# Combinations of w_in and low halves of x on GpSimd, with a new order of work, in an attention and MoE kernel on one core

## The chip, the core and the metric

The kernel runs on one core of a Trainium2 chip. A core has five engines that matter here, each with its own queue of instructions that it executes strictly in order: TensorE (PE in the profile, with its weight loads as PEld), VectorE (DVE), ScalarE (ACT), GpSimd (POOL) and SyncE (SP), from which nearly all DMA transfers are issued. Engines wait for one another by semaphores. The metric is the device time of one execution in microseconds (us), from the first to the last instruction and what lies around them; lower is better.

## The reference

Attention with positive random features over 8 batches, 8 heads, 576 tokens and 64 channels, followed by a feed-forward layer with an unusual gate:

```python
def phi(x):
    proj = np.einsum('bhsd,df->bhsf', x, w_phi)
    proj = proj - np.max(np.abs(proj), axis=-1, keepdims=True)
    return np.concatenate([np.exp(proj), np.exp(-proj)], axis=-1)
q_p, k_p = (phi(q), phi(k))
kv = np.einsum('bhsf,bhsd->bhfd', k_p, v)
num = np.einsum('bhsf,bhfd->bhsd', q_p, kv)
den = np.einsum('bhsf,bhf->bhs', q_p, np.sum(k_p, axis=2))[..., None] + 1e-06
x = num / den            # to (4608 tokens, 512)
h = x @ w_in             # w_in 512 x 2048
sp = np.maximum(h, 0.0) + np.log1p(np.exp(-np.abs(h)))
g = h * erf(sp)
out = g @ w_out          # w_out 2048 x 512
```

## The kernel before

**Precision.** The large products run on TensorE in float16. Each float32 operand is split in two float16 parts, a high half (the rounded value, made by ScalarE or by a cast on VectorE) and a low half (value minus high half, one subtraction), and a product takes three matmuls: high by high, high by low, low by high.

**The first product** x @ w_in is done with seven products of blocks in place of eight (a scheme of Strassen's kind). It needs combinations of blocks of w_in and of blocks of x. The combinations of w_in are made once: the columns are handled in four units u = 0 to 3, each in two row blocks j = 0, 1. `split_weights(u, j)` (line 503) loads two tiles with `single` (line 474, which assembles float32 words from loaded 64-bit ones with three operations on lines 478, 480 and 482), makes four differences of 128x256 elements with the helper `tt` (line 520, called four times, so 32 in all), and then turns seven forms into high halves (an ACT operation recorded on line 442) and low halves (lines 530 and 531). The forms of unit 0 stay in SBUF (tile `wi`); those of units 1 to 3 are written to DRAM and fetched again for every stage.

**The stages.** x comes in nine stages s = 0 to 8 (eight batches of 512 tokens, and one stage of the 64 left-over tokens of each batch). For each stage, `split(s, f, ...)` (line 778) is called for seven forms f: the high half is cast on line 783 (ACT, stages 0 and 1) or 785 (DVE), the low half is subtracted on line 788 (128x512 elements), and SyncE issues a transposing DMA (line 789) that lays the result into an `x` tile. Some combinations of x are made by `combine` (line 812). A kind `x` of tiles may hold at most XS slots at once. The attention of pairs of heads p runs beside the products of earlier stages; from pair 12 on, q and k are split too, by `halve(p, i)` (line 598; low half on line 606, two per pair).

**Who does what.** Constants at the top choose the engine. `X_POOL = 0, 3` puts the low halves of x of stages 0 to 2 on GpSimd and the others on VectorE. `HL_POOL = 8, 16` puts the low halves of q and k of pairs 12 to 15 (the split starts at 12) on GpSimd. `T_POOL = 4` tells that the differences of w_in of all four units count as GpSimd's. But the helper `tt` refers to the variable `eng` of `split_weights`, and the loop below it assigns that variable anew, before any instruction is issued:

```python
pool = u < T_POOL
eng = nc.gpsimd if pool else nc.vector
tt = lambda ...: op(POOL if pool else DVE, 750 if pool else 330, lambda: eng.tensor_tensor(...), ...)
...
for f, x, c, key in (...):
    ...
    pool = u in LI_POOL and f in LF_POOL      # LI_POOL is empty
    eng = nc.gpsimd if pool else nc.vector
```

So the order of work is laid out as if GpSimd made the 32 differences in 750 ns each, and the instructions are issued on VectorE at those places in its queue.

**The order of work.** Every operation is first entered in a plan (`Plan.op`, line 149) with an engine, a counted length in ns, its reads and writes, and a priority (a position along TensorE's work, moved by offsets). `Plan.run` (line 199) then simulates the engines with these lengths, picks the next operation by time and priority, gives out tile slots, and issues all instructions in the order of planned start. An operation marked `port=True` may not start in the plan while one on the other of VectorE and GpSimd that is so marked is running. Where the plan expects a hole of more than 600 ns on TensorE, it fills it with pairs of matmuls on constant data (`warm`, line 1178), which compute nothing that is used. TensorE's work has three modes of how the array is used, and the plan adds 92 ns at a change and a penalty to the priority of an operation that would change it: STAY (1500) in the first steps, STAY2 (9000) in steps after N1. The weights are loaded one item at a time by `load_weight` (line 485), up to W_EARLY of them during the attention of the first batch, with a position moved by W_OFF; one of the steps of the product then follows another (`moe_step`, line 1088).

Of the kernel before, what the change touches and what calls it, by code (L numbers as in the profile page):

```python
# [13 lines left out]
ALU = mybir.AluOpType  # L14
# [25 lines left out]
PE_TURNED = 10  # L40
SPEED = {}
STAY2 = 9000.0
N1 = 9
TWO = 36
ATTN = 5
QK_POOL = 0, 0
W_POOL = 0, 0
GATE_AT = 0.0, 0.0, 0.0
X_POOL = 0, 3
T_POOL = 4  # L50
LO_POOL = ()
LI_POOL = ()
LF_POOL = 0, 1, 2, 3, 4, 5, 6
XC_POOL = 0, 0
HL_POOL = 8, 16
LATE = 1500.0
FIRST = 2
XS = 12
XT = 3
RES = 1  # L60
WS = 8
# [2 lines left out]
BIG = 20  # L64
HALF = 22
N0 = 6
W_EARLY = 4
W_NS = 1600.0
W_NS2 = 9000.0
ACC_AHEAD = 5000.0  # L70
# [6 lines left out]
W_FROM = 14  # L77
W_EACH = 7
W_MM = 14
W_OFF = 5000.0  # L80
W_AHEAD = 12000.0
X_AHEAD = 4000.0
SEVEN = 7
# [39 lines left out]
class Plan:  # L123
# [22 lines left out]
    def buf(self, kind):  # L146
        return Buf(self, kind)

    def op(self, eng, cost, fn, r=(), w=(), done=None, off=0.0, mode=COLS, land=0.0, port=False, need=None, give=None):
        o = Op()  # L150
        o.eng, o.cost, o.fn, o.mode, o.land, o.port = eng, cost, fn, mode, land, port
        o.slack = self.slack
        o.need, o.give = need, give
        o.stay = self.stay
        o.done = cost + 120.0 if done is None else done
        o.prio = self.pos + off
        o.seq = len(self.ops)
        o.succ, o.unmet, o.ready, o.start = [], 0, 0.0, None
        o.bufs = []
        deps = {}  # L160

        def touch(item, write):
            b, key = item if isinstance(item, tuple) else (item, None)
            if b not in o.bufs:
                o.bufs.append(b)
                b.left += 1
            known = write
            for k, (ws, rs) in b.state.items():
                if k is None or key is None or k == key:
                    known = True  # L170
                    for d in ws:
                        deps[d] = True
                    if write:
                        for d in rs:
                            deps[d] = True
            assert known, "read before it is written"
            if write:
                if key is None:
                    b.state.clear()
                b.state[key] = ([o], [])  # L180
            else:
                b.state.setdefault(key, ([], []))[1].append(o)

        for item in r:
            touch(item, False)
        for item in w:
            touch(item, True)
        deps.pop(o, None)
        for d in deps:
            d.succ.append(o)  # L190
        o.unmet = len(deps)
        self.ops.append(o)
        return o
# [125 lines left out]
def favor_attention_moe(ctx: ExitStack, tc: tile.TileContext, qk, vp, wphi, w_in, w_out, out):  # L319
# [6 lines left out]
    def slots(group, n, shape, dt):  # L326
        for i in range(n):
            plan.slot(group, f"{group}{i}", sb.tile(shape, dt, tag=f"{group}{i}", name=f"{group}{i}"))
# [48 lines left out]
    slots("half", HALF, [P, 512], F32)  # L377
    plan.kind("x", "half", (("x",), XS))
    plan.kind("xt", "half", (("xt",), XT))
# [24 lines left out]
    op, buf = plan.op, plan.buf  # L404
    PE, DVE, ACT, POOL, SP = "PE", "DVE", "ACT", "POOL", "SP"
# [52 lines left out]
    def wform(u, f):  # L458
        if u < RES:
            b = const[f"wi{u}"]  # L460
            return b, f, lambda hl, j: b.t[:, f, hl, j, :]
        b = wforms[u][f // 2]
        return b, f, lambda hl, j: b.t.bitcast(F16).rearrange("p (f h j n) -> p f h j n", f=2, h=2, j=2)[:, f % 2, hl, j, :]
# [21 lines left out]
    def load_weight():  # L485
        item = wq.pop(0)
        loaded.add(item)
        at_pos = plan.pos
        plan.pos += W_OFF
        if item[0] == "o":  # L490
# [12 lines left out]
    def split_weights(u, j):  # L503
        if u >= RES and j == 0:
            wforms[u] = [buf("ws") for _ in range(4)]
        rows = []
        for c in (j, 2 + j):
            st, f = buf("wr"), buf("wf")
            src = []
            for i in range(2):  # L510
                cols = slice(2 * (i * 8 + 2 * u) * P, 2 * (i * 8 + 2 * u + 2) * P)
                src.append((lambda st, i=i: st.t.bitcast(I32)[:, i * 512 : i * 512 + 512], w_in[c * P : (c + 1) * P, cols]))
            single(src, SP, st, f)
            rows.append(f)
        a, b = rows
        s, t = buf("wf"), buf("wf")
        lo, hi = slice(0, Q), slice(Q, 2 * Q)
        pool = u < T_POOL
        eng = nc.gpsimd if pool else nc.vector
        tt = lambda o, oc, x, xc, y, yc, r: op(POOL if pool else DVE, 750 if pool else 330, lambda: eng.tensor_tensor(o.t[:, oc], x.t[:, xc], y.t[:, yc], op=ALU.subtract), r=r, w=[(o, oc.start)], port=True)  # L520
        tt(s, lo, a, hi, a, lo, [a])
        tt(s, hi, b, hi, a, hi, [a, b])
        tt(t, lo, b, hi, s, lo, [b, (s, 0)])
        tt(t, hi, b, lo, t, lo, [b, (t, 0)])
        for f, x, c, key in ((B11, a, lo, a), (T3, s, hi, (s, Q)), (B21, b, lo, b), (T2, t, lo, (t, 0)), (T1, s, lo, (s, 0)), (B22, b, hi, b), (T4, t, hi, (t, Q))):
            w, k, view = wform(u, f)
            act(340, lambda view=view: view(0, j), lambda x=x, c=c: x.t[:, c], AF.Copy, [key], [(w, (k, j, 0)) if u < RES else (w, (f, j))], scale=SWI)
            pool = u in LI_POOL and f in LF_POOL
            eng = nc.gpsimd if pool else nc.vector
            op(POOL if pool else DVE, 800 if pool else 330, lambda eng=eng, view=view, x=x, c=c: eng.scalar_tensor_tensor(  # L530
                view(1, j), x.t[:, c], SWI, view(0, j), op0=ALU.mult, op1=ALU.subtract), r=[key, (w, (k, j, 0)) if u < RES else (w, (f, j))], w=[(w, (k, j, 1)) if u < RES else (w, (f, j))], port=True)
        if u >= RES and j == 1:
            wstored[u] = []
            for i in range(4):
                d = buf("wd")
                d.left += 1
                w = wforms[u][i]
                n = 512 * min(2, FORMS - 2 * i)
                op(SP, 430, lambda d=d, w=w, n=n: nc.sync.dma_start(d.t[:, :n], w.t[:, :n]), r=[w], w=[d], done=4000, land=1300 * LAND * n / 512)
                wstored[u].append(d)  # L540
# [57 lines left out]
    def halve(p, i):  # L598
# [4 lines left out]
        op(ACT, 100 + 0.85 * n, lambda: nc.scalar.copy(hv()[:, 0, cols], src.t[:, cols]), r=[src], w=[(hl, (i, 0))], off=-AHEAD)  # L603
        pool = HL_POOL[0] <= p < HL_POOL[1]
        eng = nc.gpsimd if pool else nc.vector
# [172 lines left out]
    def split(s, f, view, reads):  # L778
        t, x = buf("xt"), buf("x")
        xs[s, f] = x  # L780
        tv = lambda i: t.t.bitcast(F16).rearrange("p (t i d) -> p t i d", t=2, i=2)[:, :, i, :]
        if XT_ACT[0] <= s < XT_ACT[1]:
            op(ACT, 540, lambda: nc.scalar.copy(tv(0), view()), r=reads, w=[(t, 0)])
        else:
            op(DVE, 350, lambda: nc.vector.tensor_copy(tv(0), view()), r=reads, w=[(t, 0)], port=True)
        pool = X_POOL[0] <= s < X_POOL[1]
        eng = nc.gpsimd if pool else nc.vector
        op(POOL if pool else DVE, 1400 if pool else 600, lambda: eng.tensor_tensor(tv(1), view(), tv(0), op=ALU.subtract), r=[*reads, (t, 0)], w=[(t, 1)], port=True)
        op(SP, 1280, lambda: nc.sync.dma_start_transpose(
            x.t.bitcast(F16).rearrange("p (n t) -> p n t", t=P), t.t.bitcast(F16)), r=[t], w=[x], done=3100, land=600)  # L790
        if 1 < FIRST and s < FIRST:
            d = xds[s, f] = buf("xd")
            op(SP, 430, lambda: nc.sync.dma_start(d.t, x.t), r=[x], w=[d], done=4000, land=1300 * LAND, off=3000.0)
# [18 lines left out]
    def combine(s, out, x, y, sub, r, w):  # L812
        pool = XC_POOL[0] <= s < XC_POOL[1]
        eng = nc.gpsimd if pool else nc.vector
        op(POOL if pool else DVE, 1400 if pool else 600, lambda: eng.tensor_tensor(out(), x(), y(), op=ALU.subtract if sub else ALU.add), r=r, w=w, port=True)

    def first_half(s, a, ka):
        split(s, A11, d3(flat(a, 0)), ka)
# [311 lines left out]
    for i, x in enumerate(att):  # L1130
        if x < 0:
            break
        plan.pos += x
        if i > W_FROM and i % W_EACH == 0 and len(loaded) < W_EARLY:
            load_weight()
# [9 lines left out]
    for n, (h, o) in enumerate(steps):  # L1145
        plan.slack = SLACK if n > N0 else SLACK0
        plan.stay = STAY2 if n > N1 else STAY
        b = next((i for i, s in enumerate(starts) if s > n), None)
# [6 lines left out]
        while h and (h[0] < B and h[1] == 0 and (h[0], A22) not in xs or h[0] == B and h[1] == 0 and (B, A22) not in xs):  # L1155
            y = next(att)
            plan.pos += max(y, 0.0)
        for x in moe_step(h, o):
# [8 lines left out]
            while owed > 0:  # L1167
                y = next(att, None)
# [18 lines left out]
    t = plan.run(warm)  # L1187
# [47 lines left out]
```

## Time and profile before

| what | value |
|---|---|
| median of 3 runs | 968.59 us (968.54 to 968.77) |
| the profiled execution's own time | 968.28 us |
| its span | 966.5 us |
| mean granted clock of TensorE | 0.999 |
| DMA traffic | 170.82 MB |
| ACT busy | 681.9 us (71%) |

In the profile, a group of instructions is given by its line in the kernel, its engine and operation, the tiles written and read and the shape. Where a helper records an operation, the line is the helper's (424 for all products, 434 for the attention's products with v and with kv, 633 for its projections, 442 for most ACT operations). The instructions of VectorE overlap by some 0.09 us in their records, so the spacing of the starts, not the recorded duration, is what one of them takes of the engine. A wait is put down to the instruction that ended last before it.

### The profile page before, as it was taken

To read this page: it belongs to the slowest core of one execution; us is meant where nothing else is said; L and a number is where in the kernel's file an instruction comes from. 1 tells how busy PE (TensorE), PEld (TensorE's weight loads), DVE (VectorE), ACT (ScalarE), POOL (GpSimd) and SP (SyncE) were. 2 spreads that over 40 slices of the span, in tenths; PEclk is the share of its full clock that TensorE was granted. 3 is DMA by queue.
4 is the path that set the end of the run, shared out by engine and by line. 5 is a ranking of instruction groups with operands and counts; after the bars stand their busy time and mean duration, and the time that the engine had idled before them with its cause. 6 is when DMAs were issued, how large, how long until landed. Compare 5 with 4: busy or idle time off the path is not lost.

```text
span 966.5 us, 35295 instructions
## 1 busy us (share of the span) xinstructions
PE 947.7 (98%) x15806; PEld 754.5 (78%) x15806; DVE 752.7 (78%) x1351; ACT 681.9 (71%) x1000; POOL 43.9 (5%) x35
## 2 busy tenths in 40 slices
PE   9989989899999999999999999999999999999998
PEld 7878867768777878788787878787878787887875
DVE  6999999999977896898888886889896754335442
ACT  7877888777877576957687766766666755657571
POOL 0021100131310000000000000000000000000000
PEclk9999999999999999999999999999999999999999
DMA  9489999699855766386948493596735863342112
GB/s 330 113 217 307 271 283 289 240 324 304 175 164 159 186 123 205 84 212 148 224 120 196 127 221 101 142 223 166 164 69 148 219 153 132 110 144 89 56 56 77
DMA packets 173336, 170.82 MB, mean 177 GB/s; under 512 B 124544, under 2 KB 125696, under 8 KB 173184
## 3 DMA queue, kind: packets, MB, share of 16 engines
q1 hardware_dynamic: 173184, 168.57, 64.9%
q8 instruction: 123, 2.02, 0.9%
q14 instruction: 29, 0.24, 0.1%
HBM read 110.07 MB, written 29.10 MB: 144 GB/s over the span
## 4 chain that ended last, share of the span: by engine, by line
PE 78%; DVE 3%; issue 0%; DVEq 0%
PE bank L424 65%; PE bank L434 9%; PE bank L633 4%; DVE gl L1034 0%; DVE m L581 0%; DVE half L482 0%; DVE big L530 0%; DVE big L592 0%; DVE half L480 0%; DVE big L964 0%; DVE half L520 0%; DVE big L1030 0%; DVE uq L592 0%; DVE big L754 0%; DVE half L478 0%
## 5 line engine op out<-in xcount | busy, mean ns | idle before, releaser
L424 PE MATMUL bank<-half,big 128*64 128x256 f16 x4536 | 274.1, 273 | 3.4 <-DVE big L964 2.3
L424 PEld LDWEIGHTS <-big 128*64 128x64 f16 x4536 | 247.7, 110 | 22.8 <-issue 4.5
L442 ACT ACTIVATE big<-bank 128x512 f32<-128x512 f32 x190 | 111.1, 603 | 143.7 <-PE bank L424 140.5
L424 PE MATMUL bank<-woh,gh 128*64 128x512 f16 x1024 | 199.1, 380 | 2.3 <-ACT gh L1033 2.3
L424 PE MATMUL bank<-woh,gl 128*64 128x512 f16 x1024 | 198.6, 380 | 1.2 <-DVE gl L1034 1.2
L424 PE MATMUL bank<-wol,gh 128*64 128x512 f16 x1024 | 198.9, 379 | 0.0
L442 ACT ACTIVATE big<-big 128x512 f32<-128x512 f32 x206 | 127.6, 628 | 71.0 <-DVE big L592 35.0
L424 PEld LDWEIGHTS <-gh 128*64 128x64 f16 x2048 | 119.2, 110 | 74.7 <-ACT gh L1033 2.9
L964 DVE SCALAR_TENSOR_TENSOR big<-bank,big 128x512 f32<-128x512 f32 x108 | 73.9, 686 | 71.6 <-PE bank L424 67.0
L1030 DVE TENSOR_TENSOR big<-big,big 128x1024 f32<-128x1024 f32 x72 | 86.2, 1221 | 32.5 <-ACT big L1026 32.4
L581 DVE TENSOR_REDUCE m<-bank 128x4 f32<-128x512 f32 x144 | 92.7, 684 | 21.7 <-PE bank L633 21.5
L424 PEld LDWEIGHTS <-gl 128*64 128x64 f16 x1024 | 61.3, 110 | 45.9 <-DVE gl L1034 1.7
L424 PE MATMUL bank<-half,wi 128*64 128x256 f16 x1512 | 93.3, 273 | 1.2 <-DVE big L964 0.7
L1034 DVE TENSOR_TENSOR gl<-big,gh 128x1024 f16<-128x1024 f32 x64 | 80.4, 1265 | 13.5 <-ACT gh L1033 13.5
L424 PEld LDWEIGHTS <-wi 128*64 128x64 f16 x1512 | 81.4, 110 | 6.3 <-issue 1.9
L434 PE MATMUL bank<-kv,big 128*64 128x65 f32 x2304 | 84.6, 222 | 0.0
L434 PEld LDWEIGHTS bank<-v,big 128*64 128x64 f32 x2016 | 77.2, 137 | 8.0 <-ACT big L442 0.9
L434 PE MATMUL bank<-v,big 128*64 128x65 f32 (+1 forms) x2016 | 82.1, 228 | 0.3 <-ACT big L442 0.3
L434 PEld LDWEIGHTS bank<-kv,big 128*64 128x64 f32 x2304 | 78.6, 138 | 4.2 <-issue 0.2
L1010 ACT ACTIVATE big<-big 128x1024 f32<-128x1024 f32 x72 | 72.6, 1050 | 0.8 <-DVE big L964 0.4
L1033 ACT CAST gh<-big 128x1024 f16<-128x1024 f32 x64 | 65.5, 1039 | 4.0 <-DVE big L1030 3.9
L592 DVE TENSOR_TENSOR uq<-bank,m 128x512 f32<-128x512 f32 x72 | 49.2, 683 | 0.6 <-PE bank L664 0.5
(69 smaller groups left out, 1127.3 us busy)
## 6 DMA issues: line engine op xcount, KB each, us to landing
big<-wd SPq DMA_DIRECT2D x81, 512.0 KB, 5.0
ld<-in_qk_dram SPq DMA_DIRECT2D x31, 576.0 KB, 4.8
part<-half SPq DMA_DIRECT2D x36, 256.0 KB, 3.5
half<-part SPq DMA_DIRECT2D x36, 256.0 KB, 3.3
v<-in_vp_dram SPq DMA_DIRECT2D x28, 325.0 KB, 4.0
big<-in_moe_w_in_dram SPq DMA_DIRECT2D x32, 256.0 KB, 5.3
big<-in_moe_w_out_dram SPq DMA_DIRECT2D x16, 512.0 KB, 5.8
out_dram<-half SPq DMA_DIRECT2D x32, 256.0 KB, 2.3
```

What stands on the lines that cost most here:

```text
L424: nc.tensor.matmul(o[half], a[:, half], b, start=start, stop=stop, **kw)
L434: nc.tensor.matmul(o[half], a[:, half], b, start=first and c == 0, stop=last and c == 1)
L442: nc.scalar.activation(out_(), in_(), func, **k)
L581: op(DVE, 600, lambda: nc.vector.tensor_reduce(m.t, ps(), axis=AX.X, op=ALU.max, apply_absolute_value=True), r=[b], w=[m])
L592: op(DVE, 600, lambda: nc.vector.tensor_tensor(to(), ps(), m.t.unsqueeze(2).to_broadcast([P, GT, NF]), op=ALU.subtract), r=[b, m], w=[key])
L633: nc.tensor.matmul(both[nm].t[:, t * P : (t + 1) * P], x()[rows], w.t[rows, :], start=i == 0, stop=i == len(terms) - 1)
L964: op(DVE, 640, lambda: nc.vector.scalar_tensor_tensor(h.t[:, c * 512 : c * 512 + 512], b.t, HSCALE, h.t[:, c * 512 : c * 512 + 512], op0=A ...
L1010: fn = lambda: nc.scalar.activation(L.t, h.t, AF.Softplus, scale=1.0 / SG)
L1030: op(DVE, 1140, lambda h=h, L=L: nc.vector.tensor_tensor(h.t, h.t, L.t, op=ALU.mult), r=[L, h], w=[h], port=True, off=GATE_OFF[0] * (v + 1))
L1033: op(ACT, 940, lambda h=h, a=a: nc.scalar.copy(halfs(a), h.t), r=[h], w=[a], off=GATE_OFF[1] * (v + 1))
L1034: op(DVE, 1140, lambda h=h, a=a, b=b: nc.vector.tensor_tensor(halfs(b), h.t, halfs(a), op=ALU.subtract), r=[h, a], w=[b], port=True, off=G ...
```

## The change

Six constants change, the engine of `tt` is bound when the helper is defined, and the lengths that the plan counts for GpSimd's subtractions become smaller: 640 for 750 in `tt`, 1160 for 1400 in `split` and `combine`. The 32 differences of w_in go to GpSimd. With X_POOL up to 9, the low halves of x of all nine stages do (63, where 21 did). With HL_POOL up to 12, GpSimd makes no low half of q or k any more; VectorE makes the eight of pairs 12 to 15. XS goes from 12 to 10, W_EARLY from 4 to 3, W_OFF from 5000 to 4000 and N1 from 9 to 3. As all operations are placed by one plan, the order on every engine is made anew. DMA transfers are the same in number and size.

```diff
-N1 = 9
+N1 = 3
-X_POOL = 0, 3
+X_POOL = (0, 9)
 T_POOL = 4
-HL_POOL = 8, 16
+HL_POOL = (8, 12)
-XS = 12
+XS = 10
-W_EARLY = 4
+W_EARLY = 3
-W_OFF = 5000.0
+W_OFF = 4000.0
...
-        tt = lambda o, oc, x, xc, y, yc, r: op(POOL if pool else DVE, 750 if pool else 330, lambda: eng.tensor_tensor(o.t[:, oc], x.t[:, xc], y.t[:, yc], op=ALU.subtract), r=r, w=[(o, oc.start)], port=True)
+        tt = lambda o, oc, x, xc, y, yc, r, eng=eng: op(POOL if pool else DVE, 640 if pool else 335, lambda: eng.tensor_tensor(o.t[:, oc], x.t[:, xc], y.t[:, yc], op=ALU.subtract), r=r, w=[(o, oc.start)], port=True)
...
-        op(POOL if pool else DVE, 1400 if pool else 600, lambda: eng.tensor_tensor(tv(1), view(), tv(0), op=ALU.subtract), r=[*reads, (t, 0)], w=[(t, 1)], port=True)
+        op(POOL if pool else DVE, 1160 if pool else 600, lambda: eng.tensor_tensor(tv(1), view(), tv(0), op=ALU.subtract), r=[*reads, (t, 0)], w=[(t, 1)], port=True)
...
-        op(POOL if pool else DVE, 1400 if pool else 600, lambda: eng.tensor_tensor(out(), x(), y(), op=ALU.subtract if sub else ALU.add), r=r, w=w, port=True)
+        op(POOL if pool else DVE, 1160 if pool else 600, lambda: eng.tensor_tensor(out(), x(), y(), op=ALU.subtract if sub else ALU.add), r=r, w=w, port=True)
```

## The prediction

> **What bounds the kernel now.** The first page gives the span and the busy time of each engine:
>
> ```profile
> span 966.5 us, 35295 instructions
> PE 947.7 (98%) x15806; PEld 754.5 (78%) x15806; DVE 752.7 (78%) x1351; ACT 681.9 (71%) x1000; POOL 43.9 (5%) x35
> ```
>
> TensorE is busy for 98% of the span, so all that another engine can give back lies in the other 18.8 us, and in matmuls that do no work. Where these lie is seen in the table of stretches (busy time of each engine, number of instructions, granted clock, DMA):
>
> ```profile
> core 0: us, PE busy (x) PEld busy (x) DVE busy (x) ACT busy (x) POOL busy (x), PEclk, DMA share, GB/s
> 0.00:30.00 30.00, 28.55 (x480) 22.73 (x482) 21.46 (x51) 21.00 (x65) 0.70 (x6) 1.00 0.81 289
> 30.00:210.00 180.00, 167.50 (x3004) 137.96 (x3006) 177.42 (x389) 146.75 (x300) 29.58 (x20) 1.00 0.89 254
> 210.00:260.00 50.00, 50.00 (x880) 41.05 (x878) 48.80 (x78) 43.38 (x58) 9.92 (x6) 1.00 0.97 267
> 260.00:300.00 40.00, 40.00 (x624) 29.42 (x622) 29.50 (x47) 25.04 (x34) 3.73 (x3) 1.00 0.63 160
> 300.00:750.00 450.00, 449.66 (x8076) 355.88 (x8073) 376.24 (x673) 317.97 (x410) 0.00 (x0) 1.00 0.65 159
> 750.00:940.00 190.00, 189.96 (x2556) 153.42 (x2554) 91.23 (x111) 122.82 (x133) 0.00 (x0) 1.00 0.42 121
> ```
>
> There are two kernels here. From 30 to 210 us VectorE is busy 177.4 of 180 us and TensorE idles 12.5 us; from 210 to 940 us TensorE idles less than half a microsecond, whatever VectorE does. The chain that ended last says the same: it runs on VectorE until 202.84 us, and on TensorE from there.
>
> ```profile
> 199.17 1.55 DVE half L482
> 200.73 2.11 DVE gl L1034
> 202.84 0.04 issue
> 202.88 8.19 PE bank L424 x84
> ```
>
> In the first of the two stretches there are also matmuls on constant data, put in where the plan expected holes (line 1178 alone, PE then PEld):
>
> ```profile
> 30.00:210.00 180.00, 6.47 (x48) 2.41 (x48) 1.00 0.89 254
> ```
>
> So at most 12.5 + 6.5 = 19.0 us can go, from 30 to 210 us, and that takes VectorE off the path there. The rest of the idle time is the start (1.45 us) and the end (4.4 us after 940), which the change doesn't touch.
>
> **The change part by part. The 32 differences of w_in leave VectorE.** Their rows and two of them with what follows on VectorE:
>
> ```profile
> L520 DVE TENSOR_TENSOR half<-half,half x24: 397/419/1118, 27.5 to 188.6; 128x256 f32<-128x256 f32 x24
> L520 DVE TENSOR_TENSOR half<-half x8: 396/421/425, 25.0 to 184.5; 128x256 f32<-128x256 f32 x8
> 30.00:210.00 180.00, 13.06 (x29) 1.00 0.89 254
> 187.07 0.43 DVE L520 TENSOR_TENSOR half<-half,half 128x256 f32<-128x256 f32 x1
> 187.41 1.29 DVE L581 TENSOR_REDUCE m<-bank 128x4 f32<-128x512 f32 x2
> ```
>
> The next one starts 0.34 us on, though 0.43 us is recorded: records overlap by 0.09. 29 lie in the full stretch (the third row is line 520 alone there), so VectorE gains 29 x 0.335 = 9.7 us. The three before 30 us count as nothing: VectorE is busy 21.5 of 30 us there.
>
> **What GpSimd gives back.** GpSimd's subtractions of twice the size, and of the halves of q and k:
>
> ```profile
> L788 POOL TENSOR_TENSOR half<-big,half x18: 1154/1173/5371, 39.2 to 260.7; 128x512 f16<-128x512 f32 x18
> L606 POOL TENSOR_TENSOR ld<-ld,ld x8: 1159/1400/1601, 169.5 to 287.6; 128x640 f16<-128x640 f32 x4, 128x512 f16<-128x512 f32 x4
> ```
>
> One of 256 elements is in no row; half of the median is 0.59, the change's own count is 0.64, and I take 0.64. It isn't free for VectorE. Beside GpSimd's work, single VectorE instructions are held: the rows of GpSimd from 169 us on, and VectorE's beside them,
>
> ```profile
> 169.53 1.40 POOL L606 TENSOR_TENSOR ld<-ld,ld 128x640 f16<-128x640 f32 x1 [43.98 <-ACT ld L603]
> 170.09 1.12 DVE L520 TENSOR_TENSOR half<-half,half 128x256 f32<-128x256 f32 x1
> 172.25 1.20 POOL L606 TENSOR_TENSOR ld<-ld,ld 128x512 f16<-128x512 f32 x1 [1.32 <-ACT ld L603]
> 172.37 1.37 DVE L530 SCALAR_TENSOR_TENSOR big<-half,big 128x256 f16<-128x256 f32 x1
> 198.78 2.96 POOL L606 TENSOR_TENSOR ld<-ld,ld 128x640 f16<-128x640 f32 x2
> 199.09 1.64 DVE L482 SCALAR_TENSOR_TENSOR half<-big,half 128x512 int32<-128x512 int32 x1
> 200.65 2.17 DVE L1034 TENSOR_TENSOR gl<-big,gh 128x1024 f16<-128x1024 f32 x1
> ```
>
> against medians of 0.42, 0.42, 0.68 and 1.22 us of the same lines (0.419 above for line 520):
>
> ```profile
> L530 DVE SCALAR_TENSOR_TENSOR big<-half,big x42: 384/422/1368, 65.9 to 192.1; 128x256 f16<-128x256 f32 x42
> L482 DVE SCALAR_TENSOR_TENSOR half<-big,half x32: 674/684/1639, 21.9 to 254.5; 128x512 int32<-128x512 int32 x32
> L1034 DVE TENSOR_TENSOR gl<-big,gh x64: 1185/1220/2243, 126.6 to 875.8; 128x1024 f16<-128x1024 f32 x64
> ```
>
> They are held 0.70, 0.95, 0.96 and 0.95: 3.56 us for four GpSimd instructions of 5.6 us (a share of 0.64). Beside the 16 low halves of x before 210 us there are six such places, the first and the second of them
>
> ```profile
> 51.58 0.72 DVE L520 TENSOR_TENSOR half<-half,half 128x256 f32<-128x256 f32 x1
> 58.86 1.13 DVE L584 TENSOR_SCALAR mb<-m 128x4 f32<-128x4 f32 x1
> ```
>
> (0.30 and 0.97 us over the usual 0.42 and 0.16), with 0.97, 0.54, 0.82 and 0.05 after them: 3.65 us for 16 x 1.16 = 18.6 us, a share of 0.20. Other kinds are never held: of the two rows that follow, the first has its longest at seven times its median, the second (a reduction out of PSUM) at 12 ns above it.
>
> ```profile
> L584 DVE TENSOR_SCALAR mb<-m x18: 158/162/1133, 7.6 to 90.7; 128x4 f32<-128x4 f32 x18
> L581 DVE TENSOR_REDUCE m<-bank x144: 674/682/694, 6.4 to 721.4; 128x4 f32<-128x512 f32 x144
> ```
>
> A GpSimd instruction thus costs VectorE nothing where VectorE has instructions of the second kind to run beside it, and up to its own length where it hasn't. The 29 differences put 29 x 0.64 = 18.6 us on GpSimd in the stretch; at the mean share, 7.2 / 24.2 = 0.30, they cost VectorE 5.6 us; at the shares of the two kinds 3.7 and 11.9. I take 5.6, and keep both ends.
>
> The Trainium skill, "SBUF — State Buffer", section "Who interferes with whom", says that VectorE and GpSimd share a pair of ports under an exclusive lock, and that a VectorE instruction with two SBUF inputs, or in a two-port mode, is blocked for the whole of a GpSimd instruction that reads SBUF, whichever starts first winning. The rows above agree in kind (a write of four columns, line 584, took 1.13 us). By that page the share would be anything up to 1, which is the slower rival below.
>
> **The low halves of q and k of pairs 12 and 13** come back to VectorE in the stretch, those of 14 and 15 after it. VectorE's own rows for later pairs:
>
> ```profile
> L606 DVE TENSOR_TENSOR ld<-ld,ld 128x640 f16<-128x640 f32 x16 | 13.1, 819 | 0.4 <-ACT ld L603 0.4
> L606 DVE TENSOR_TENSOR ld<-ld,ld 128x512 f16<-128x512 f32 x16 | 10.9, 683 | 0.0
> ```
>
> Less the overlap that is 2 x 0.73 + 2 x 0.60 = 2.7 us, against 3.56 us of holding that ends: a gain of 0.9. The other four fall at 225 to 290 us, where TensorE doesn't idle: nothing.
>
> **The 42 low halves of x of stages 3 to 8** leave VectorE after 300 us. It saves 42 x 0.60 = 25 us there and is held 42 x 1.16 x 0.30 = 15 us; TensorE's work covers either, as 376 of 450 us are busy now. If that cover were short (share 0.64: 31 us held, 6 lost in all) VectorE would still stand under 86%. The danger is a late x tile: GpSimd's longest instruction took 5.37 us where 1.16 is usual, 4.2 more. Line 788 before the product of the next stage, then the first use of `wi` in that product:
>
> ```profile
> 360.00:370.00 10.00, 0.69 (x1) 0.00 (x0) 1.00 1.14 265
> 370.00:380.00 10.00, 1.06 (x18) 0.95 (x20) 0.00 (x0) 0.00 (x0) 1.00 0.75 253
> ```
>
> The last low half is some 8 us or more ahead of the first form's product, and its own comes later still. I cost it at nothing. The transposing DMAs stay 63; SyncE waits for GpSimd in place of VectorE there, and the loads behind them in its queue wait as long, up to those 4.2 us; they are issued ahead, and no wait of TensorE names a DMA.
>
> **The order and the constants.** The plan counted, in the stretch, 29 x 0.75 + 16 x 1.40 + 6.6 (four halves by its formula) = 50.7 us of GpSimd's work, in which VectorE might do no port work; now 29 x 0.64 + 16 x 1.16 = 37.1, or 27% less. Its expected holes, and the matmuls that fill them, should shrink: between nothing and all of the 6.5 us, and I take 27%, 1.7 us. W_EARLY moves one item of weights from early to later; yet the first operation of `single` ran six times before 60 us, two to an item, three items:
>
> ```profile
> 0.00:60.00 60.00, 2.50 (x6) 1.00 0.71 227
> ```
>
> so I cost it at nothing (5 us of VectorE, 6 x 0.6 + 2 x 0.33 + its forms, if the fourth item did run ahead). N1 keeps TensorE longer in one mode in steps 4 to 9, for changes of some 0.1 us while it idles anyway: nothing. XS, two x tiles fewer, takes from the 8 us of lead: nothing, up to 4 us if each of the stages waited half a microsecond.
>
> **The sum**, for the profiled execution's 968.28 us (966.5 of span and 1.8 around it): -9.7 + 5.6 - 0.9 = -5.0 us of VectorE, which TensorE can use one for one, as 5.0 is less than the 12.5 it idles; -1.7 of filling. 968.28 - 6.7 = 961.6. The median stands 0.3 above that execution: **961.9 us**.
>
> **The rivals.**
>
> *Port lock, slower.* In 30 to 210 us the 29 differences hold VectorE for a share s of their length. The saving is 9.7 + 0.9 = 10.6 us, the price 18.6 s, so it decides at s = 0.57. For it speak the four rows of 0.64 and that line 530 and the next item's lines 480 and 482, all of them kinds that were held, follow in the queue; against it the 0.20 of the 16 others. At s = 0.75 to 1 the loss is 3.3 to 8.0 us: 972 to 977 us.
>
> *A wait in place of the work, no change.* The differences depend on one another: the fourth needs the third, and that the first. Four in a row take 2.6 us on GpSimd and 1.3 on VectorE, and ACT's casts and line 530 wait behind them; VectorE, in order, would stand still 8 x 1.2 = 9.8 us at most, half of it being enough to eat the 5.0. Against it: VectorE has other items' work to place between. 967 to 970 us. That the change doesn't do what it says (GpSimd's instructions not growing) would also end here.
>
> *Nearly all of it goes.* With differences in the shadow of PSUM work (s near 0) and a plan whose lengths are right, 10.6 us and most of the filling go: 951 to 955 us. Against it, no row has a share below 0.20.
>
> **How the numbers follow.** Forecast (955 to 966.6) 0.52; nearly all 0.12; no change 0.14; slower 0.22. About 0.2%, 1.9 us, is what a measurement of this kernel tells from no change. So faster 0.64, same 0.14, slower 0.22. The range leaves out the last of either side: s = 0 with all the filling gone gives 951.5, s = 0.75 gives 972. I take 952 to 972; the forecast's own is 955 to 967.
>
> **What would show it.** Right: line 520 on GpSimd 32 times near 0.64 us; GpSimd at 6 + 63 + 32 = 101 instructions; TensorE's idle time in 30 to 210 us down from 12.5 to about 7, its filler below 48 matmuls; the chain leaving VectorE before 200 us; nothing new after 300 us. Wrong: VectorE rows of 1 us and more beside each GpSimd difference (port lock); line 530 or ACT waiting for line 520 with VectorE idle (the wait); TensorE idle after 300 us in front of a product (late x, a mistake in my slack).

## The result and the profile after

| | before | after |
|---|---|---|
| median of 20 runs each, us | 968.76 (967.24 to 969.89) | 970.43 (968.64 to 971.96) |
| ratio after / before | | 1.0017, 95% interval 1.001 to 1.0024 |
| the profiled execution: time, span, us | 968.28, 966.5 | 971.43, 969.5 |

The change makes the kernel slower by 0.17%, about 1.7 us, where 6.7 us of gain were forecast. Two later executions at a low granted clock, one of e2 (1393.1 us, clock 0.655) and the profiled one of e18 (1572.2 us, 0.578), are in no ratio below, and e18 has no figure of work. The first page of the changed kernel:

```profile
span 969.5 us, 35327 instructions
PE 952.0 (98%) x15796; PEld 745.7 (77%) x15796; DVE 742.2 (77%) x1285; ACT 680.7 (70%) x1000; POOL 124.3 (13%) x101
```

The change did what it says: 101 instructions on GpSimd (35 before), 66 fewer on VectorE, whose busy time falls by 10.5 us. TensorE is busy 4.3 us *longer*, with ten instructions fewer. Where, the table of stretches says (columns as in the prediction: busy time of each engine, then granted clock):

```profile
0.00:30.00 30.00, 28.55 (x476) 22.86 (x478) 20.83 (x49) 20.92 (x66) 3.69 (x10) 1.00 0.79 284
30.00:210.00 180.00, 169.05 (x2936) 139.04 (x2934) 174.66 (x356) 143.03 (x297) 53.18 (x44) 0.98 0.87 256
210.00:260.00 50.00, 49.46 (x836) 39.46 (x836) 48.65 (x84) 41.04 (x55) 6.25 (x4) 1.00 0.85 238
260.00:300.00 40.00, 40.00 (x666) 32.53 (x664) 28.35 (x44) 28.11 (x35) 1.16 (x1) 1.00 0.66 166
300.00:750.00 450.00, 449.97 (x8086) 356.17 (x8084) 371.78 (x642) 317.05 (x411) 43.36 (x31) 1.00 0.67 161
```

From 30 to 210 us TensorE idles 10.95 us (12.5 before), but executes 2936 instructions where it executed 3004, and its clock is 0.98 (1.00 before). From 300 us on TensorE idles as little as before (0.03 us up to 750, 0.34 before). VectorE is relieved of 29 differences and is still busy 174.7 of 180 us.

A measure that all runs share is the *useful work* of TensorE done by 210 us: matmuls counted by shape, filler left out, each shape at its spacing in the trace (0.0545 us for 256 float16 columns and for 130 float32, 0.108 for 512, 0.029 for 65 float32, 0.068 and 0.0325 for a projection's 128 in float32 and float16, 0.147 for a transposition). It is 175.6 us before and 172.6 after, and the profiled executions took 968.3 and 971.4: the sum is 1144 in both, so nearly the whole difference is made before 210 us. The figure belongs to the profiled execution alone, which can lie some us off the median (965.66 against 967.49 us for e1, 975.93 against 971.51 for e2). In the sixteen other kernels that have this number below, the sum lies at 1143 to 1149.

### The profile page after: what moved, and what is told of

The parts are those of the page before. It is cut to its first block, busy times and chain, and to the rows that moved or that the text cites. A ratio compares the mean times of both kernels' runs of the same rounds, so it can differ in the third digit from the quotient of the medians.

```text
span 969.5 us, 35327 instructions
## 1 busy us (share of the span) xinstructions
PE 952.0 (98%) x15796; PEld 745.7 (77%) x15796; DVE 742.2 (77%) x1285; ACT 680.7 (70%) x1000; POOL 124.3 (13%) x101
## 3 DMA queue, kind: packets, MB, share of 16 engines
q8 instruction: 123, 2.02, 0.9%
## 4 chain that ended last, share of the span: by engine, by line
PE 86%; DVE 8%; ACT 4%; issue 1%; DVEq 0%; ACTq 0%
PE bank L424 67%; PE bank L434 12%; PE bank L633 5%; DVE big L530 2%; ACT big L442 1%; PE bank L664 1%; DVE m L581 1%; DVE gl L1034 1%; PE bank L1178 1%; DVE half L480 1%; DVE big L964 1%; DVE half L482 1%; ACT big L1010 0%; ACT L1024 0%; DVE wol L497 0%
## 5 line engine op out<-in xcount | busy, mean ns | idle before, releaser
L424 PEld LDWEIGHTS <-gh 128*64 128x64 f16 x2048 | 115.3, 110 | 75.6 <-issue 1.1
L788 POOL TENSOR_TENSOR half<-big,half 128x512 f16<-128x512 f32 x54 | 76.0, 1419 | 636.5 <-DVE half L785 498.0
```

Of the source, the lines that this page charges most:

```text
L424: nc.tensor.matmul(o[half], a[:, half], b, start=start, stop=stop, **kw)
L788: op(POOL if pool else DVE, 1160 if pool else 600, lambda: eng.tensor_tensor(tv(1), view(), tv(0), op=ALU.subtract), r=[*reads, (t, 0)], w ...
```

## The experiments

Eighteen kernels were run, each in rounds with the kernel before on the same chip. Ratios are to the kernel before, with 95% intervals. "In its own order" means that the plan is untouched and only the engine that executes an instruction differs at its place; everything else makes the order anew.

| run | what it is | median, us | ratio (interval) | work by 210 us, profiled execution |
|---|---|---|---|---|
| e1_bind_only | order of before, differences on GpSimd | 967.49 | 0.9979 (0.9967 to 0.9992) | 177.6 |
| e2_after_tt_dve | order of after, differences on VectorE | 971.51 | 1.0033 (1.0018 to 1.0048) | 169.3 |
| e3_no_tt_before | order of before, no differences | 963.22 | 0.9952 (0.9939 to 0.9966) | 180.3 |
| e4_no_tt_after | order of after, no differences | 964.03 | 0.9952 (0.994 to 0.9964) | 180.1 |
| e12_after_tt_unread | order of after, differences made, nobody reads them | 971.02 | 1.002 (1.0011 to 1.003) | 174.7 |
| e6_after_x_dve | order of after, late low halves of x on VectorE | 971.91 | 1.0031 (1.002 to 1.0042) | 174.5 |
| e17_after_hl_in_place | order of after, q/k low halves on GpSimd | 971.71 | 1.0039 (1.0026 to 1.0051) | 170.8 |
| e11_bind_x_pool | order of before, differences and all of x on GpSimd | 965.44 | 0.9959 (0.9947 to 0.997) | 176.9 |
| e18_bind_x_hl | order of before, every move of the change | 966.41 | 0.9975 (0.9964 to 0.9986) | |
| e5_after_old_consts | after with the four constants of before | 972.33 | 1.0036 (1.0024 to 1.0048) | 175.1 |
| e7_dve_counted | before, differences counted on VectorE | 977.05 | 1.0075 (1.0057 to 1.0093) | 168.5 |
| e9_bind_lengths | before, bound, new lengths | 971.93 | 1.0032 (1.002 to 1.0044) | 174.9 |
| e10_after_hl_pool | after, q/k low halves on GpSimd, re-ordered | 969.22 | 1.0005 (0.9996 to 1.0013) | 176.4 |
| e16_after_short_lengths | after, counted at 500 and 900 | 972.62 | 1.0044 (1.0032 to 1.0057) | 175.7 |
| e13_after_old_lengths | after, counted at 750 and 1400 | 974.31 | 1.0064 (1.0051 to 1.0076) | 168.6 |
| e14_after_long_lengths | after, counted at 900 and 1650 | 978.71 | 1.0104 (1.009 to 1.0118) | 166.6 |
| e15_after_old_lengths_hl | e13 with q/k low halves on GpSimd | 978.76 | 1.0107 (1.0091 to 1.0122) | 167.7 |
| e8_fill | after, 17 pairs of filler at two waits | 973.18 | 1.0045 (1.0033 to 1.0057) | |

**The move or the order?** The kernel before with only the engine bound:

```diff
-        tt = lambda o, oc, x, xc, y, yc, r: op(
+        tt = lambda o, oc, x, xc, y, yc, r, eng=eng: op(
```

> The kernel before with the engine of the 32 differences of w_in bound, and nothing else: the order is that of before, since the plan's lengths and constants are untouched; only the engine that executes the 32 differences differs. Theory A (GpSimd hands the saving back: VectorE is held by the shared port and waits for the differences in its queue): 967 to 971 us, no change against before, with VectorE's rows of line 530 held by up to 1 us beside line 520 on GpSimd. Rival B (the move gains what the prediction said, and the new order and its constants lose it): 962 to 965 us.

The changed kernel with the differences put back on VectorE at their places:

```diff
-        tt = lambda o, oc, x, xc, y, yc, r, eng=eng: op(
+        tt = lambda o, oc, x, xc, y, yc, r, eng=nc.vector: op(
```

> The changed kernel in its own order, but the 32 differences executed by VectorE at the places where the order counts them as GpSimd's (as the kernel before did with its order). Theory A (executing them on GpSimd is worth little): within 2 us of the changed kernel, 969 to 973. Rival B (the move is worth some 5 to 7 us and the order loses it): 975 to 978 us.

And both orders without the differences, whose readers take the loaded tiles:

```diff
-... lambda: eng.tensor_tensor(o.t[:, oc], x.t[:, xc], y.t[:, yc], op=ALU.subtract), r=r, ...
+... lambda: None, r=r, ...
+            y = {id(s): a, id(t): b}.get(id(x), x)
-            act(340, lambda view=view: view(0, j), lambda x=x, c=c: x.t[:, c], ...
+            act(340, lambda view=view: view(0, j), lambda x=y, c=c: x.t[:, c], ...
```

> The kernel before in its own order without the 32 differences: they are not executed at all, and the forms that would read them read the loaded tiles instead, so the weights' forms are other numbers and all other work is the same. It bounds what taking 10.7 us off VectorE can give when nothing is given back. If the load of VectorE sets the pace until 203 us: 958 to 961 us. If the places and the waits of the order set it: 965 to 968 us.

> The changed kernel in its own order without the 32 differences (left out as in the run before this one). Theory A (GpSimd's execution costs VectorE holds and waits): 961 to 965 us, at least 5 below the changed kernel. Rival B (the new order is what loses): 967 to 970, within 3 of the changed kernel.

967.5, 971.5, 963.2 and 964.0 us: e1, e2 and e4 lie where theory A puts them, but it isn't the whole. Taking the ratios, the move in the order of before gains 2.0 us, half of what the prediction gave it (4.1). In the order of after it gains about as little, 1.6 (1.0033 to 1.0017, the intervals overlapping). Between e1 and the changed kernel stand 3.7 us that the rest of the change loses, so the order isn't innocent either. And without the differences both orders are equally fast: the new order is bad only with the differences in it, on either engine.

What VectorE's relief can give at most is the run without them (e3), which came out between the two expectations: 10.7 us of VectorE's work (32 x 0.335) are worth 4.6 us (0.48%). The chain of waits of that run, from 170 to 215 us, shows what is late next: ScalarE (lines from 530 on stand one number higher in this kernel; the ACT lines without a tile are loads of activation tables, 1.28 us each),

```profile
by line: PE bank L424 39.0%; ACT big L442 9.1%; DVE big L1031 4.8%; issue 4.6%; ACT big L1011 4.5%; DVE half L480 4.0%; DVE big L531 3.5%; PE bank L634 3.4%; PE bank L434 3.4%; ACT L1011 2.9%; ACT L1027 2.9%; ACT L1025 2.9%; DVE m L582 2.7%
```

with its activations and the loading of their tables on the path beside VectorE.

**Held by the port, or waiting for the difference?** In the order of after, GpSimd executes the differences and nothing reads them (edit as above, with the differences left in):

> The changed kernel in its own order, GpSimd executing the 32 differences, but the forms of w_in reading the loaded tiles in their place, so that nothing waits for a difference (the weights' forms are other numbers). Without the differences it had been 964.0 us, with them 970.4. If VectorE's being held by the port is the cost: 968 to 971 us, with line 530 held as in the changed kernel. If the wait for the differences (ScalarE's casts and line 530 behind them) is the cost: 963.5 to 966 us.

971.0 us: as slow as the changed kernel. The wait for the results costs nothing that can be seen; that GpSimd executes them costs it, 6.6 us against e4. The groups of line 530 on VectorE from 30 to 210 us, with the differences, with them unread, and without them (busy, mean ns):

```profile
L530 DVE SCALAR_TENSOR_TENSOR big<-half,big 128x256 f16<-128x256 f32 x42 | 21.3, 556 | 0.6 <-ACT big L442 0.6
```

```profile
L531 DVE SCALAR_TENSOR_TENSOR big<-half,big 128x256 f16<-128x256 f32 x42 | 20.5, 536 | 0.4 <-ACT big L442 0.3
```

```profile
L531 DVE SCALAR_TENSOR_TENSOR big<-half,big 128x256 f16<-128x256 f32 x42 | 17.3, 462 | 0.5 <-ACT big L442 0.4
```

The same instructions take 3 to 4 us more beside GpSimd. Summed over all groups of VectorE in the stretch (mean less the usual duration, times count), it is held 11.6, 11.1 and 6.1 us: the differences hold it 5.0 to 5.5 us. Two things bound this reading. In the order of before, e1 is held as long as the changed kernel (11.4 us in each, summed instruction by instruction; 7.6 in e3, so that the differences hold it 3.8 there) and yet is 3.7 us faster: more holding is not what the new order loses by. And the hold is not the only way in which GpSimd's work can cost time. The differences also stand in GpSimd's queue among the low halves of x, and SyncE, which issues the DMAs of these, waits for them (us in total, times, longest; from 30 to 210 us of the changed kernel):

```profile
SPq L789 <- POOL half L520: 5.1, 2, 4.9
```

In e12 the same wait is as long (5.5 us), in e1 it is 0.8. No run parts it from the hold, so that the hold is the whole cost of GpSimd's work isn't shown.

How the two engines stop one another is seen once in each direction. GpSimd at 165 us, and VectorE beside it:

```profile
165.68 4.94 POOL L520 TENSOR_TENSOR half<-half 128x256 f32<-128x256 f32 x1 [9.55 <-DVE half L482]
```

```profile
165.47 0.68 DVE L480 SCALAR_TENSOR_TENSOR half<-big,half 128x512 int32<-128x512 int32 x1
166.07 1.21 DVE L1030 TENSOR_TENSOR big<-big,big 128x1024 f32<-128x1024 f32 x1
167.21 0.68 DVE L482 SCALAR_TENSOR_TENSOR half<-big,half 128x512 int32<-128x512 int32 x1
167.81 1.21 DVE L1034 TENSOR_TENSOR gl<-big,gh 128x1024 f16<-128x1024 f32 x1
168.95 1.08 DVE L530 SCALAR_TENSOR_TENSOR big<-half,big 128x256 f16<-128x256 f32 x3
169.95 0.68 DVE L964 SCALAR_TENSOR_TENSOR big<-bank,big 128x512 f32<-128x512 f32 x1
```

Five kinds with two inputs from SBUF (seven instructions) run back to back, and GpSimd's subtraction, 0.73 us when nothing hinders it, ends at 170.62, beside the first instruction that reads PSUM. The Trainium skill, "SBUF — State Buffer", section "Who interferes with whom", tells of one lock on the shared ports, held for a whole instruction, that a VectorE instruction with at most one SBUF input, outside the two-port modes, doesn't need. The trace agrees: VectorE's line 530 is held beside GpSimd's work, and here GpSimd beside VectorE's, through a whole row of instructions.

**The other moves.** The late low halves of x back on VectorE at their places, in the order of after:

```diff
-        eng = nc.gpsimd if pool else nc.vector
+        eng = nc.gpsimd if pool and s < 3 else nc.vector
```

> The changed kernel in its own order, but the low halves of x of stages 3 to 8 executed by VectorE at their places. All lie after 300 us, where TensorE hardly idles: by that reading within 1 us of the changed kernel, 969.5 to 971.5. If GpSimd's low halves delayed x or held VectorE to TensorE's cost: 966 to 969.

and all of them on GpSimd, with the differences, in the order of before:

```diff
         pool = X_POOL[0] <= s < X_POOL[1]
-        eng = nc.gpsimd if pool else nc.vector
+        eng = nc.gpsimd
```

> The kernel before in its own order, with the 32 differences and the low halves of x of all nine stages executed by GpSimd at their places. The differences alone gave 967.5 us. If the late low halves give the 1.4 us that they gave in the changed kernel's order: 966 us, and the fastest of the right kernels so far. If they give nothing, as predicted: 967 to 968.5.

971.9 (1.0031 against 1.0017; above both of its ranges) and 965.4 us (0.9959 against 0.9979): the move of the late halves is worth 1.4 and 1.9 us, the intervals of each pair just overlapping. For the first there is a place in the trace: with them on VectorE (e6), TensorE idles 1.5 us from 300 to 750 us, where the changed kernel idles 0.03, and waits for VectorE (us in total, times, longest):

```profile
PE bank L633 <- DVE big L592: 1.3, 2, 0.7
```

For the second there is none, as e1 doesn't idle there. Of the kernels that do all of the work, e11 is the fastest, 0.41% below the kernel before.

The low halves of q and k, on GpSimd in the order of after, then on VectorE in the order of before with the other moves:

```diff
         pool = HL_POOL[0] <= p < HL_POOL[1]
-        eng = nc.gpsimd if pool else nc.vector
+        eng = nc.gpsimd if p < 16 else nc.vector
```

> The changed kernel in its own order, with the low halves of q and k of pairs 12 to 15 executed by GpSimd at their places, as before the change. By the prediction's term their place on VectorE gains 0.9 us: 971 to 971.5 us here. If their return to VectorE loses what the re-ordered run showed (969.2 with them on GpSimd against 970.4): 969 us.

> The order of before, with the 32 differences and all low halves of x executed by GpSimd, and the low halves of q and k by VectorE: every instruction on the engine that the change gives it, in the order of before. The same with the low halves of q and k on GpSimd took 965.4 us. If the three moves gain what they gained apart and the new order is what loses: 964 to 967 us. If the moves together lose: 969 to 971, as the changed kernel.

In the order of after their return to VectorE gains 2.1 us (1.0039 to 1.0017, the intervals apart), in the order of before it loses 1.5 (0.9959 to 0.9975, the intervals overlapping). With re-ordering, e10 (`HL_POOL = (8, 16)` in the changed kernel) has them gain on GpSimd:

> The changed kernel with the low halves of q and k of pairs 12 to 15 on GpSimd as before, order made anew. By the prediction's term (0.9 us gained by their return to VectorE): 971 to 972 us. If their return is what loses: 966 to 969.

969.2 us. The sign of this term depends on the order around it; it isn't settled. But e18 settles the larger question: *every* move of the change, in the order of before, gives 0.9975. The new order turns that into 1.0017, a loss of 0.42%, 4.1 us, with the intervals well apart.

**Which part of the new order?** The four constants, the lengths, or the truth of the count:

```diff
-N1 = 3
+N1 = 9
-XS = 10
+XS = 12
-W_EARLY = 3
+W_EARLY = 4
-W_OFF = 4000.0
+W_OFF = 5000.0
```

> The changed kernel with N1, XS, W_EARLY and W_OFF as before (9, 12, 4, 5000); engines and lengths as changed, order made anew. The move alone, in the order of before, had given 967.5 us against 968.4. If the four constants lose the 3 us between that and the changed kernel: 966 to 968 us. If the new lengths or the other moves (low halves of x, of q and k) lose them: 969 to 972.

The kernel before with the engine bound, 640 for 750 and 1160 for 1400:

> The kernel before with the engine bound and the new lengths (640, 1160), order made anew with them, all other constants as before. The move alone gave 967.5 us, the changed kernel 970.4. If the order that these lengths make is what loses: 970 to 973 us. If the moves of the low halves are: 965 to 968.

The kernel before with `T_POOL = 0`, so that the plan knows that VectorE makes the differences:

> The kernel before with the 32 differences on VectorE and counted there (330 ns each in place of 750 on GpSimd), all other constants as before: the order is made anew with the truth about where they run. If an order that fits is what counts: 963 to 966 us. If VectorE's load is what counts, the same as before: 967 to 970. If a new order alone costs something: 970 to 973.

972.3, 971.9 and 977.1 us, the last above all of its ranges. The four constants by themselves aren't the loss (with the old ones it is 1.8 us worse). The new lengths, with the old constants, make an order that is 5.1 us slower than that of e1, which is laid out with 750 and 1400 (1.0032 against 0.9979). The true count for VectorE makes one that is 7.3 us slower than the kernel before. In that one the plan expects more holes, and fills them (line 1178 alone, from 30 to 210 us: TensorE busy and count, before it was 6.47 and 48):

```profile
30.00:210.00 180.00, 16.10 (x136) 7.30 (x136) 0.98 0.83 252
```

So I formed the theory that longer counts help where GpSimd makes the differences, and ran the changed kernel with other lengths, e13 as here, e14 with 900 and 1650, e16 with 500 and 900, e15 as e13 with `HL_POOL = (8, 16)`:

```diff
-op(POOL if pool else DVE, 640 if pool else 335, ...
+op(POOL if pool else DVE, 750 if pool else 335, ...
-op(POOL if pool else DVE, 1160 if pool else 600, ...
+op(POOL if pool else DVE, 1400 if pool else 600, ...
```

> The changed kernel with GpSimd's subtractions counted at the lengths of before (750 and 1400 for 640 and 1160), order made anew, all else as changed. The order made with the new lengths had lost 4 to 5 us against that of before (972 against 967.5, all differences on GpSimd in both). If the lengths lose it, because a longer count keeps VectorE's port work off the places where GpSimd runs: 964 to 968 us. If any new order loses it: 969 to 973.

> The same with lengths of 900 and 1650, longer than GpSimd's instructions are. If a longer count is what helps: as the run before or less, 963 to 968 us, with VectorE held for less than the 11.5 us of the changed kernel in 30 to 210 us. If it is the order as such, in no relation to the lengths: anywhere from 966 to 973, and the two runs need not agree.

> The changed kernel with the lengths of before and the low halves of q and k of pairs 12 to 15 on GpSimd as before. If both steps that had lost time are independent: 1 us less than with the lengths alone, 963 to 967 us. If the order as such decides: no relation, 966 to 973.

> The changed kernel with GpSimd's subtractions counted shorter than they are (500 and 900), order made anew. Counted at 640, 750 and 900 for the small ones it had taken 970.4, 974.3 and 978.7 us. If time follows the count, a tight order losing less than one with room in it: 964 to 968 us. If 640 is nearest to what the machine does and so is best: 971 to 976. If there is no relation: anywhere from 966 to 978.

That theory fell. Counted at 500, 640, 750 and 900 it takes 972.6, 970.4, 974.3 and 978.7 us; from 640 to 750 it loses 4.6 us with the constants and moves of the change, where it wins 5.1 without them (e9 to e1). e13, e14 and e15 came out above every range that their expectations name. Nor is 640 the truer length: the small subtraction takes 0.73 us when nothing hinders it, to which 750 is nearer; the 1160 for the large one is right. The counted length has no effect of its own that these runs show; each set of numbers makes another order, and nine orders with the differences on GpSimd (e1, e5, e9, e10, e13, e14, e15, e16 and the changed kernel) spread over 967.5 to 978.8 us with the same work done. What an order is worth wasn't to be had from its inputs.

**The clock.** In the changed kernel the granted clock falls to a half twice before 210 us (columns to POOL busy, then the clock):

```profile
60.00:61.00 1.00, 0.52 (x4) 0.33 (x4) 1.00 (x3) 0.00 (x0) 1.00 (x2) 1.00 0.96 381
61.00:62.00 1.00, 1.00 (x12) 1.00 (x13) 1.00 (x3) 0.00 (x0) 1.00 (x2) 0.58 1.27 272
62.00:63.00 1.00, 1.00 (x8) 0.62 (x6) 1.00 (x3) 0.72 (x2) 1.00 (x2) 0.50 1.13 246
63.00:64.00 1.00, 1.00 (x6) 0.72 (x4) 1.00 (x2) 0.36 (x2) 0.52 (x1) 0.50 1.48 239
64.00:65.00 1.00, 1.00 (x13) 0.81 (x14) 0.73 (x2) 1.00 (x6) 0.00 (x0) 0.71 0.66 207
```

and again right after the wait that ends VectorE's part of the chain, where TensorE has idled 2.25 us:

```profile
192.26 1.20 DVE m L581 x2
193.46 0.61 DVE big L592
194.07 0.04 issue
194.11 0.58 PE bank L434 x8
194.69 3.50 PE bank L424 x30
```

```profile
190.00:195.00 5.00, 2.75 (x38) 1.53 (x36) 5.00 (x9) 2.21 (x4) 1.21 (x1) 0.93 0.72 287
195.00:200.00 5.00, 5.00 (x82) 4.09 (x80) 3.52 (x6) 3.42 (x6) 0.00 (x0) 0.73 1.03 250
```

To keep TensorE busy, filler pairs were put into its queue, meant for the front of the work behind these waits (in the part left out here, `FILL` lists each place, as a count of issued matmuls, and the pairs that go there):

```diff
+            if pe and spare and fill and COUNT[0] >= fill[0][0]:
+                for _ in range(fill.pop(0)[1]):
+                    filler(self.slots[spare[0]])
             fn()
```

> The changed kernel with 17 pairs of matmuls on constant data put into TensorE's queue at the waits behind which the granted clock was halved (7 pairs around 59 us, 10 pairs, 2.2 us, in front of the wait that ended at 194.1 us). If the halved clock after 194 us is on the path: 1.5 to 2 us less than the changed kernel, 968 to 969, with the clock at 1.0 through 190 to 200 us. If it is covered by other waits: within 0.5 us of the changed kernel, 970 to 971.

It took 973.2 us, 2.7 more than the changed kernel. The fillers ran *behind* the waits: the seven pairs around 61 us waited 1.3 us themselves for VectorE to empty a bank, and the clock was halved there as before; the ten pairs, 2.16 us, ran from 195.94 us on, behind a wait of 2.36 us. But that wait left the clock alone:

```profile
195.00:200.00 5.00, 4.77 (x72) 3.57 (x74) 3.73 (x6) 2.69 (x5) 0.00 (x0) 1.00 0.98 298
```

So the two kernels price the second halving all the same. The first work behind the wait and the next products with v, in the changed kernel and here (where all matmuls are recorded on line 419):

```profile
194.11 0.58 PE L434 MATMUL bank<-kv,big 128*64 128x65 f32 x8 [2.25 <-DVE big L592]
198.02 1.10 PE L434 MATMUL bank<-v,big 128*64 128x65 f32 x32
```

```profile
195.23 0.45 PE L419 MATMUL bank<-kv,big 128*64 128x65 f32 x8 [2.36 <-DVE big L612]
199.63 1.10 PE L419 MATMUL bank<-v,big 128*64 128x65 f32 x32
```

TensorE does the same work between the two, without a pause, in 3.91 us at the halved clock and in 4.40 - 2.16 = 2.24 us at the full one. The halving cost 1.7 us of TensorE's time, and from there to 940 us TensorE idles only 0.6 us in which some of that could be hidden.

What the first halving cost, with waits on either side of it, remains open. And the clock isn't what parts good orders from bad: before 210 us it was halved for 3.4 us once in e13's profiled execution (974.5 us) and for 6.8 us in e10's (968.6), and not at all in the kernel before, e1, e3 and e4. Within e1, the six runs with a mean clock of 1.0 have a mean of 965.8 us and the three at 0.997 to 0.998 one of 968.4; among the changed kernel's own runs there is no such relation.

## Why the prediction was wrong

**The bound** was read rightly in the main: nearly all of the difference is made before 210 us. That nothing after 300 us costs anything holds of the changed kernel, not of every order: e6 idles 1.5 us there.

**"TensorE can use one for one"** failed. It was argued from 12.5 us of idle time being more than the 5.0 saved. With 10.7 us taken off VectorE and nothing given back (e3), the time fell by 4.6 us, 0.43 for one: ScalarE's activations and table loads stand on the path beside VectorE's work, and the chain, followed back only from its last wait, had shown VectorE alone.

**The price of holding** came out near, in part by luck. 0.30 of 18.6 us, 5.6, was forecast; 5.0 to 5.5 was measured in the new order and 3.8 in that of before. A difference takes 0.73 us on GpSimd and not 0.64 (no row had shown one, and half of the larger one's time was no measure of it), so the 28 in the stretch come to 20.4 us and the share to 0.25 to 0.27, or 0.19: two errors of opposite sign. And a microsecond of holding has no fixed price either: in the order of after, the differences on GpSimd cost 6.6 us (e4 to e12) where they hold VectorE for 5.0, in the order of before 2.6 us (e3 to e1) where they hold it for 3.8.

**The sum of the moves** was forecast at -5.0 us and is -2.4 in the order of before (e18). Its sign held, its size was half. Late low halves of x were costed at nothing and gave 1.4 to 1.9; those of q and k were costed at -0.9 and came out at +1.5 and -2.1 in the two orders.

**The step that turned the sign is "The order and the constants".** It gave -1.7 us, by the fall of GpSimd's counted work, and put a change of every engine's order at nothing beyond that; the measured value is +4.1 (e18 to the changed kernel). The filler did shrink, as that step said. Line 1178 alone in the changed kernel, from 30 to 210 us:

```profile
30.00:210.00 180.00, 4.46 (x38) 2.09 (x38) 0.98 0.87 256
```

38 matmuls, 48 before. But a plan's expected holes are a small part of what an order does. Against e1, which has the same differences on GpSimd, TensorE does 4.3 us less useful work from 30 to 210 us (152.1 against 156.4; these two profiled executions lie 5.8 us apart, the kernels by their ratios 3.7). The row of that stretch in e1:

```profile
30.00:210.00 180.00, 168.71 (x3038) 138.59 (x3035) 174.90 (x359) 147.34 (x301) 54.35 (x48) 1.00 0.93 263
```

The halved clock makes up 3.4 of the 4.3 (two times 1.7, from the rows above); 2.3 is time of TensorE that is neither work nor filler nor idle (9.4 us, against 7.1 in e1; between 30 and 210 us the matmuls change between the three modes of the array 84 times, 71 in e1); 1.1 less of filler (0.216 a pair) and 0.3 less of idle time work the other way. The account closes. Of its causes, the second halving is shown (by the rows of e8); the price of the first and the changes of mode are only argued, and what made this order meet them is open.

**The rivals.** 970.4 us lies just above the range of the second one, "no change" at 967 to 970 us, and below that of the first, 972 to 977. The second one's mechanism wasn't it: the wait for the differences costs nothing (e12). The mechanism that the rows show at work is the first one's, the port, but at a share below 0.30 and not at the 0.57 that it needed; the loss came from the order, for which no rival stood.

## What to carry to other kernels

When a change moves work *and* makes the order anew, measure the two apart: execute the moved work at its old places first. A plan that was told where the differences really run gave an order 7 us slower here (e7), other counted lengths one 5 us slower (e9), and no input of the plan told which order would be good. And an engine's share of the chain of waits is no rate of exchange: take the work out altogether, once, and see what its absence is worth before paying for its move.

## What the runs showed of the hardware

- The granted clock went to a half after TensorE had idled 2.25 us in one piece, and at 61 us after several pieces of 0.2 to 1.2 us; it stayed there for 3.4 us (by the rows above 0.84 of the first microsecond, two whole ones, and 0.58 of the last). Waits of 2.36 us in e8 and of 2.02 us in the kernel before (at 136.8 us) left it at 1.00. The Trainium skill, "TensorE: Matmul & The Clock Gate", tells of a free-running window of about 3.4 us (section "What's actually happening") and advises against gaps of over 3 us (section "Why this matters for your kernels"). The length of the slow piece agrees; the harmless length of a gap doesn't, as 2.25 us was enough once.
- A subtraction of 128x256 float32 elements on GpSimd takes 0.72 to 0.73 us when unhindered, not half of the 1.16 of 128x512, and up to 4.94 us beside VectorE's instructions with two inputs from SBUF (the changed kernel):

```profile
L520 POOL TENSOR_TENSOR half<-half,half x24: 719/732/2706, 27.5 to 183.2; 128x256 f32<-128x256 f32 x24
L520 POOL TENSOR_TENSOR half<-half x8: 727/1117/4937, 23.0 to 180.3; 128x256 f32<-128x256 f32 x8
```
